# Four small instructions of a recurrent-attention-plus-MLP kernel move from GpSimd to ScalarE

## The chip, the core and the metric

The kernel runs on one NeuronCore of a Trainium2 chip. The core's engines each work through a queue of their own, in order, and meet through semaphores: TensorE (PE in the profile; PEld is its weight load), VectorE (DVE), ScalarE (ACT), GpSimd (POOL) and SyncE (SP), which here only issues DMAs. The metric is the time of one execution on the device in microseconds (us).

## The reference

The first half is a recurrence with a decay for every channel, over four batches, eight heads, 768 time steps and 48 channels a head. The second half is an MLP whose activation is the maximum of two products.

```python
for t in range(S):
    cur = np.einsum('bhd,bhe->bhde', u[None] * kt, vt)
    y[:, :, t] = np.einsum('bhd,bhde->bhe', rt, state + cur)
    state = wt[:, :, :, None] * state + np.einsum('bhd,bhe->bhde', kt, vt)
...
h1 = x @ w1          # x: the 3072 rows of y, 384 wide
h2 = x @ w2          # 1024 wide
return (np.maximum(h1, h2) @ w_out).astype(np.float32)
```

## The kernel before

**Units.** The work is cut into eight units (line 39). A unit is 256 time steps of one batch (units 0 to 3, the first third of the sequence) or of two batches (unit 4: batches 0 and 1, second third; unit 5: batches 2 and 3, second third; units 6 and 7: the last third). A partition holds two neighbouring time steps, so 128 partitions hold the 256 steps, and the lower and upper 64 partitions are two chunks of 128 steps.

**A unit's steps**, by the names in the order list (`name.unit.rest`, with `@a`, `@d`, `@p` for ScalarE, VectorE, GpSimd where there is a choice):

- `load` brings w, k, r and v in. `wp` multiplies the decays of a partition's two steps, `ln` takes the logarithm (ScalarE), and `ex` sums the logarithms over time by a matmul with a triangular matrix. For units 3 to 7 that matmul runs in f16 in two parts: `hi` is the logarithm times 256, rounded to f16, and `lo` is what the rounding left, 256 times the logarithm minus `hi` (VectorE, line 398). `hi` and `lo` are written into slices of the tile that is named wst.
- `e0` and `ie` are the exponentials of the sums, `rk`, `ru`, `dg`, `dd` and `di` make the diagonal with u in it, `rw` and `kw` multiply decays into r and k, and `scale` makes the scaled r and k (tiles rp and kp). `tr` and `te` turn them (TensorE, then a ScalarE copy into the tile RK); from unit 5 on a DMA does it (`dt`).
- `kv` is the matmul of k with v, `st` adds it to the f32 state S_f, and `sm` multiplies the state with the chunk's decay, whose exponential is `we` (tile W). `sb.n.0` and `sb.n.1` round the state to bf16 for TensorE, tile S_b, one for partitions 0 to 63 and one for 64 to 127: the half-partition copies.
- `sc` is the matmul of scaled k with scaled r, `mk` copies it under a triangular mask into the tile M (VectorE, line 635), `ya` is the matmul of M with v, `yi` that of the state S_b with r, and `xe` takes the result out of PSUM.
- `gt`, `rl`, `op`, `oe` and `os` are the MLP: the matmul with w1 - w2 (line 691), relu, the matmuls with w2 @ w_out and w_out (lines 709 and 713), the copy out of PSUM and the store. The maximum of h1 and h2 is taken as relu(h1 - h2) + h2.

**What sets the order.** No scheduler is at work. The list `ORDER` (line 51) is walked once, and each step issues its instructions to the queues of its engines at that place. A wait arises where an instruction needs what another engine writes, or writes over what another still reads.

**Buffers.** In PSUM two pairs of banks, named Y, serve `kv`, `sc` and the outputs `ya`/`yi` in turn, so an `sc` waits until `mk` has read an earlier one. Four banks named G serve everything else. The tiles rku and T exist once.

**The functions in question.** `sb` (line 606) makes one instruction through the helper `copy` (line 165): 64 partitions, 192 elements each for a unit of one batch, 768 for one of two batches that carries state on. `hi` (line 392) makes one through the helper `times` (line 196): line 198 on ScalarE, line 200 on GpSimd or VectorE.

Of the kernel before, what the change touches and what calls it, by code (L numbers as in the profile page):

```python
# [53 lines left out]
mz.0.1 e0.0.1 load.0.r rw.0.0@d ex.0.0 zero.M.1@p mz.0.0 ie.0.0 ie.0.1 kw.0.0@p identb@p wt.0.0  # L54
rw.0.1@p wt.0.1 load.1.w.0 u we.0.0 identq@a uspread hot.8.3 e0.0.0 wp.1.0@p ln.1.0 ex.1.0
zero.k.1@p rk.0.0@d utake@a ru.0.0@p load.1.r rw.1.0@p load.1.v vb.1.0@a zero.M.2@p load.0.v
scale.0.1.0.0@d scale.0.1.0.1@d scale.0.0.0.0@d tr.0.0.0 vb.0.0@a vb.0.1@a kv.0 st.0.0@a sb.0.0@p
scale.0.0.0.1@d tr.0.0.1 mz.1.0 ie.1.0 dg.0 dd.0@p we.0.1 load.1.k rk.1.0@d st.0.1 kw.1.0@d ru.1.0@d
wt.1.0 di.0.0@d te.0.0.0@a hot.8.5 sc.0.0.0.0 sc.0.0.1.0 we.1.0 vb.1.1@a te.0.0.1@a hot.8.4
sc.0.0.0.1 wload.1.2 w2turn.2.0 wload.0.1 e0.1.0 zero.M.0@p sm.0@p scale.1.0.0.0@d dg.1 load.2.w.0  # L60
# [16 lines left out]
scale.4.0.0.0@d load.4.v vb.4.0@a ie.4.0 ya.2.0.1.0 vb.4.1@a yi.2.0 op.1.0 xe.2.0@a op.0.1 oe.0.1@a  # L77
ru.4.0@d scale.4.1.0.0@d tr.4.0.1 dg.4 sc.3.0.1.0 mk.3.0.1.0 sc.3.0.0.0 mk.3.0.0.0 oe.1.0@a
load.5.w.0 gt.2.0 rl.2.0@a load.3.v vb.3.1@a gt.2.3 rl.2.3@a gt.2.1 rl.2.1@a te.4.0.1@a vb.3.0@p
kv.3 st.3.0@a gt.2.2 scale.4.1.1.0@p kv.4 rl.2.2@a row.4 wp.5.0@p ln.5.0 hi.5@p dd.4@d di.4.0@d  # L80
di.4.1@d wl.3 load.5.r sb.3.0@a we.3 st.3.1 os.1.1 load.5.k sm.3@p os.0.1 load.5.v st.4.0 sb.4.0@p
rk.5.1@p ru.5.1@p tr.4.1.0 te.4.1.0@a tr.4.0.0 te.4.0.0@a op.0.0 tr.4.1.1 load.6.w.0 wp.6.0@p lo.5@d
st.4.1 rk.5.0@d ya.3.0.1.0 ex.5.1 ya.3.0.0.0 te.4.1.1@a sc.4.1.0.0 mk.4.1.0.0 sb.3.1@a yi.3.0
xe.3.0@a oe.0.0@a mz.5.1 ex.5.0 mz.5.0 op.2.1 oe.2.1@a sc.4.1.1.0 mk.4.1.1.0 sc.4.0.1.0 mk.4.0.1.0
# [18 lines left out]
xe.6.1@a ya.6.0.0.0 ya.6.0.1.0 op.5.0 scale.7.0.1.0@d dg.7 dt.7.0.1 xe.6.0@a gt.6.0 rl.6.0@d gt.6.1  # L103
rl.6.1@d gt.6.4 rl.6.4@a sm.5@p scale.7.1.1.0@p dt.7.1.1 scale.7.1.0.0@p gt.6.2 rl.6.2@d dd.7@d
vb.7.1@a gt.6.3 oe.5.0@a rl.6.3@a gt.6.6 gt.6.7 di.7.1@d rl.6.6@d gt.6.5 rl.6.5@d vb.7.0@a kv.7
st.7.0 sb.7.0@p sc.7.1.0.0 mk.7.1.0.0 rl.6.7@a op.6.0 sc.7.1.1.0 mk.7.1.1.0 dt.7.0.0 os.4.0 dt.7.1.0
op.6.2 sc.7.0.1.0 di.7.0@d mk.7.0.1.0 os.5.2 sc.7.0.0.0 mk.7.0.0.0 op.6.1 oe.6.1@d os.6.1 ya.7.1.0.0
ya.7.1.1.0 ya.7.0.0.0 ya.7.0.1.0 sb.7.1@a oe.6.0@d os.6.0 yi.7.0 yi.7.1 xe.7.0@a op.6.3 oe.6.3@a
os.6.3 os.5.3 os.5.0 oe.6.2@a xe.7.1@d gt.7.0 gt.7.7 rl.7.7@d rl.7.0@a gt.7.2 gt.7.1 rl.7.2@d gt.7.4
# [669 lines left out]
```

## Time and profile before

| | |
|---|---|
| three timed runs | 156.62, 158.8 and 159.0 us, median 158.8 |
| profiled execution | span 156.0 us from its first to its last instruction; the profile has no other time of this execution |
| busy: PE | 140.7 us, 90% of the span |
| busy: DVE | 124.1 us, 80% |
| busy: ACT | 90.0 us, 58% |
| busy: POOL | 90.4 us, 58% |
| mean granted TensorE clock | 0.985 of full speed |

The profile shows one execution. A line of the timeline is start, duration, engine, source line, operation, output <- inputs, shapes, and xN where N equal instructions follow each other; in brackets stands how long the engine was idle before it and who released it. Helpers carry the line, so line 166 is every copy on any engine and line 174 or 178 every product on VectorE or GpSimd; one goes by the tiles' names.

### The profile page before, as it was taken

How to read it: one execution, taken by the hardware profiler on the slowest of the kernel's cores; microseconds unless marked ns; L12 is line 12 of the kernel's file. 1: busy time of each engine (PE TensorE's matmuls, PEld its weight loads, DVE VectorE, ACT ScalarE, POOL GpSimd, SP SyncE). 2: the span in 40 equal slices, each digit the busy share in tenths (PEclk: the TensorE clock that was granted, in tenths of full speed). 3: DMA queues.
4: the chain of work that ended last, by engine and by line, in shares of the span. 5: the costliest groups of instructions: out<-in, count | busy, mean ns of one | idle time of the engine just before them, and what ended most of it. 6: DMA issues, size and time to landing. Idle time of an engine off the chain costs nothing.

```text
span 156.0 us, 5548 instructions
## 1 busy us (share of the span) xinstructions
PE 140.7 (90%) x2401; PEld 85.9 (55%) x2404; DVE 124.1 (80%) x161; ACT 90.0 (58%) x165; POOL 90.4 (58%) x105
## 2 busy tenths in 40 slices
PE   4899987998899989793499999999999999999991
PEld 1364645666667758561365645665556646574560
DVE  4690997999979999499989995997889987854610
ACT  3253735779979896964069689544763673023111
POOL 7949389891734975599529579486099932000000
PEclk9999999999999999999779999999999999999998
DMA  4999997999999679996098399869989298024033
GB/s 107 305 299 365 312 327 234 326 284 344 266 244 280 169 175 334 220 254 190 1 218 238 66 194 237 228 182 152 264 195 252 52 135 200 4 103 153 0 128 131
DMA packets 71187, 31.85 MB, mean 204 GB/s; under 512 B 66293, under 2 KB 70390, under 8 KB 71162
## 3 DMA queue, kind: packets, MB, share of 16 engines
q1 hardware_dynamic: 71162, 31.49, 77.3%
q8 instruction: 19, 0.31, 0.9%
q14 instruction: 6, 0.05, 0.1%
HBM read 23.61 MB, written 4.73 MB: 182 GB/s over the span
## 4 chain that ended last, share of the span: by engine, by line
PE 63%; DVE 16%; ACT 6%; issue 5%; POOL 5%; DMA 3%; SPq 1%; DVEq 0%; POOLq 0%; ACTq 0%
PE G L691 19%; PE G L713 16%; PE G L709 7%; DVE rku L174 6%; PE Y L626 4%; PE G L232 3%; PE Y L673 3%; DMA lr<-in_r_dram 3%; DVE M L635 2%; PE Y L660 2%; ACT RK L166 2%; PE Y L581 2%; POOL wst L200 1%; PE G L305 1%; POOL kp L174 1%
## 5 line engine op out<-in xcount | busy, mean ns | idle before, releaser
L691 PE MATMUL G<-xT,wd_sb 128*128 128x256 bf16 (+1 forms) x192 | 35.3, 335 | 0.7 <-ACT xT L166 0.7
L713 PE MATMUL G<-wo_sb,gT 128*128 128x384 bf16 x192 | 35.1, 326 | 0.0
L635 DVE CAST_PREDICATED M<-mask,Y 128x1024 bf16<-128x1024 int32 (+1 forms) x26 | 28.9, 1135 | 3.7 <-PE Y L626 3.6
L701 ACT ACTIVATE gT<-G 128x512 bf16<-128x512 f32 x37 | 21.0, 603 | 18.4 <-PE G L691 18.4
L691 PEld LDWEIGHTS <-wd_sb 128*128 128x128 bf16 x192 | 18.8, 101 | 13.6 <-DVE M L501 0.7
L713 PEld LDWEIGHTS <-gT 128*128 128x128 bf16 x192 | 18.7, 98 | 12.5 <-ACT gT L701 0.2
L178 POOL TENSOR_TENSOR kp<-lk,iE 128x384 bf16<-128x384 f32 x16 | 18.2, 1161 | 8.3 <-issue 4.0
L232 PE MATMUL G<-S_b 128*128 128x512 bf16 x45 | 14.6, 469 | 2.2 <-DVE S_b L261 2.1
L178 POOL TENSOR_TENSOR rku<-rku,u_b 128x384 f32<-128x384 f32 x14 | 14.0, 1025 | 4.0 <-DVE rku L174 2.2
L166 ACT COPY osb<-G 128x384 f32<-128x384 f32 x17 | 8.1, 481 | 13.7 <-PE G L713 13.4
L709 PE MATMUL G<-wc_sb,xT 128*128 128x384 bf16 x72 | 15.7, 328 | 0.0
L166 ACT CAST xT<-Y 128x768 bf16<-128x768 f32 x10 | 10.1, 1020 | 9.8 <-PE Y L660 8.2
L174 DVE TENSOR_TENSOR rku<-lr,lk 128x768 f32<-128x768 f32 x9 | 15.3, 1712 | 0.0
L626 PE MATMUL Y<-RK 48*64 48x128 bf16 x384 | 9.8, 226 | 5.1 <-DVE M L635 4.5
L166 ACT COPY RK<-G 128x1024 bf16<-128x1024 bf16 x12 | 12.0, 1026 | 1.7 <-PE G L550 1.6
L626 PEld LDWEIGHTS <-RK 48*64 48x64 bf16 x384 | 6.3, 108 | 10.5 <-issue 9.9
L425 DVE TENSOR_TENSOR MZ<-G,lg 128x384 f32<-128x384 f32 (+1 forms) x13 | 6.7, 521 | 6.0 <-PE G L383 5.1
L174 DVE TENSOR_TENSOR rp<-lr,G 128x768 bf16<-128x768 f32 (+2 forms) x13 | 10.5, 824 | 0.9 <-ACT G L421 0.6
L487 DVE TENSOR_REDUCE dg<-rku 128x16 f32<-128x768 f32 x12 | 11.0, 946 | 0.0
L178 POOL TENSOR_TENSOR lk<-lk,lw 128x384 f32<-128x384 f32 x6 | 7.3, 1226 | 5.5 <-DVE rku L174 5.5
L703 DVE TENSOR_SCALAR gT<-G 128x512 bf16<-128x512 f32 x11 | 7.4, 690 | 3.8 <-PE G L691 3.8
L232 PEld LDWEIGHTS <-S_b 128*128 128x128 bf16 x48 | 5.0, 114 | 9.6 <-issue 4.4
(102 smaller groups left out, 241.1 us busy)
## 6 DMA issues: line engine op xcount, KB each, us to landing
lk<-in_k_dram SPq DMA_DIRECT2D x12, 384.0 KB, 5.8
lr<-in_r_dram SPq DMA_DIRECT2D x12, 384.0 KB, 6.4
lv<-in_v_dram SPq DMA_DIRECT2D x12, 384.0 KB, 6.4
out_dram<-osb SPq DMA_DIRECT2D x24, 192.0 KB, 2.1
lw<-in_w_dram SPq DMA_DIRECT2D x11, 384.0 KB, 5.1
gT<-in_moe_w_dram SPq DMA_DIRECT2D x4, 512.0 KB, 6.0
wso<-in_moe_w_out_dram SPq DMA_DIRECT2D x4, 384.0 KB, 6.0
wst<-in_moe_w_dram SPq DMA_DIRECT2D x2, 512.0 KB, 5.6
```

Of the source, the lines that this page charges most:

```text
L166: (nc.scalar.copy if e == "a" else nc.vector.tensor_copy if e == "d" else nc.gpsimd.tensor_copy)(o, i)
L174: op(o, a, b)
L178: op(o[:, g], a[:, g], b[:, g])
L232: nc.tensor.matmul(t, zz[:, 0:P], zz[:, 0:512], start=True, stop=True)
L487: nc.vector.reduce_sum(s.dg[:, b].rearrange("p i h -> p h i"), s.rku[:, b], axis=AX.X)
L626: nc.tensor.matmul(t[q * Q:(q + 1) * Q, e, p * P:(p + 1) * P].rearrange("s (i g) -> s i g", i=2), s.kT[d, b, j, y * n + p, q, :], s.rT[d, ...
L635: nc.vector.copy_predicated(t[:, :, 2 * n * y:2 * n * (y + 1)].rearrange("s i (p e) g -> s p e i g", e=2), mask[:, j].bitcast(I32).unsquee ...
L691: nc.tensor.matmul(t[:, m * n * P:(m + 1) * n * P].rearrange("c (b t) -> c b t", t=P), wd_sb[:, ko, fo * P:(fo + 1) * P], s.xT[:, 0:n, ko, :],
L701: nc.scalar.activation(o, i, AF.Relu)
L703: nc.vector.tensor_scalar_max(o, i, 0.0)
L709: nc.tensor.matmul(t[:, 0:HD], s.xT[:, a, ko, :], wc_sb[:, ko, :], start=(ko == 0), stop=False)
L713: nc.tensor.matmul(t[:, 0:HD], s.gT[:, c:c + P], wo_sb[:, f, :], start=False, stop=(f == FO - 1))
```

## The change

Four steps change their engine, from GpSimd to ScalarE, and keep their place in the list: `sb.0.0`, `hi.5`, `sb.4.0` and `sb.7.0`. All other copies of the state were on ScalarE already, and of the other roundings `hi` three are on ScalarE and that of unit 7 on VectorE. Two of the four changed lines of the list:

```diff
-kv.3 st.3.0@a gt.2.2 scale.4.1.1.0@p kv.4 rl.2.2@a row.4 wp.5.0@p ln.5.0 hi.5@p dd.4@d di.4.0@d
-di.4.1@d wl.3 load.5.r sb.3.0@a we.3 st.3.1 os.1.1 load.5.k sm.3@p os.0.1 load.5.v st.4.0 sb.4.0@p
+kv.3 st.3.0@a gt.2.2 scale.4.1.1.0@p kv.4 rl.2.2@a row.4 wp.5.0@p ln.5.0 hi.5@a dd.4@d di.4.0@d
+di.4.1@d wl.3 load.5.r sb.3.0@a we.3 st.3.1 os.1.1 load.5.k sm.3@p os.0.1 load.5.v st.4.0 sb.4.0@a
```

The order on TensorE, VectorE and SyncE is the same as before. On GpSimd, at the place where units 3, 4 and 5 meet (wst is the target of `hi.5`, S_f of `sm.3`, S_b of `sb.4.0`, rku of `rk.5.1` and `ru.5.1`):

```order
 L178 TENSOR_TENSOR kp_74<-lk,iE 128x8x48 x2
 L178 TENSOR_TENSOR lg<-lw 128x384 x2
-L200 TENSOR_SCALAR wst<-lg 128x768
 L174 TENSOR_TENSOR S_f<-T,W 128x192
-L166 CAST S_b<-S_f 64x2x8x48
 L178 TENSOR_TENSOR rku<-lr,lk 128x384 x2
 L178 TENSOR_TENSOR rku<-rku,u_b 128x384 x2
```

Two instructions are gone, and the products of unit 5 follow on `sm.3`. On ScalarE at the same place (gT is a relu, lg the logarithm `ln.5`, W the exponential `we.3`, RK the three copies `te.4.1.0`, `te.4.0.0`, `te.4.1.1`):

```order
 L701 ACTIVATE gT<-G 128x512
 L372 ACTIVATE lg<-lg 128x768
+L198 ACTIVATE wst<-lg 128x768
 L166 CAST S_b<-S_f 64x4x48
 L473 ACTIVATE W<-WL 128x4
+L166 CAST S_b<-S_f 64x2x8x48
 L166 COPY RK<-G 128x4x256 x3
 L166 CAST S_b<-S_f 64x4x48
```

Here `hi.5` stands directly behind the logarithm and ahead of `we.3`, and `sb.4.0` ahead of the three copies. On ScalarE near the end of unit 7 (the second gT row is `rl.6.7`, the last relu of unit 6; the last S_b row is `sb.7.1`):

```order
 L701 ACTIVATE gT<-G 128x512
 L166 CAST vp_77<-lv 128x8x2x48
+L166 CAST S_b<-S_f 64x2x8x48
 L701 ACTIVATE gT<-G 128x512
 L166 CAST S_b<-S_f 64x2x8x48
```

`sb.7.0` now stands ahead of `rl.6.7`. In the first units, `sb.0.0` stands on ScalarE directly behind the copy `st.0.0` that it reads; on GpSimd it had stood ahead of `dd.0`.

More of the change, by code (lines that the diff above doesn't have):

```diff
@@ L56 @@
 zero.k.1@p rk.0.0@d utake@a ru.0.0@p load.1.r rw.1.0@p load.1.v vb.1.0@a zero.M.2@p load.0.v
-scale.0.1.0.0@d scale.0.1.0.1@d scale.0.0.0.0@d tr.0.0.0 vb.0.0@a vb.0.1@a kv.0 st.0.0@a sb.0.0@p
+scale.0.1.0.0@d scale.0.1.0.1@d scale.0.0.0.0@d tr.0.0.0 vb.0.0@a vb.0.1@a kv.0 st.0.0@a sb.0.0@a
 scale.0.0.0.1@d tr.0.0.1 mz.1.0 ie.1.0 dg.0 dd.0@p we.0.1 load.1.k rk.1.0@d st.0.1 kw.1.0@d ru.1.0@d
@@ L105 @@
 vb.7.1@a gt.6.3 oe.5.0@a rl.6.3@a gt.6.6 gt.6.7 di.7.1@d rl.6.6@d gt.6.5 rl.6.5@d vb.7.0@a kv.7
-st.7.0 sb.7.0@p sc.7.1.0.0 mk.7.1.0.0 rl.6.7@a op.6.0 sc.7.1.1.0 mk.7.1.1.0 dt.7.0.0 os.4.0 dt.7.1.0
+st.7.0 sb.7.0@a sc.7.1.0.0 mk.7.1.0.0 rl.6.7@a op.6.0 sc.7.1.1.0 mk.7.1.1.0 dt.7.0.0 os.4.0 dt.7.1.0
 op.6.2 sc.7.0.1.0 di.7.0@d mk.7.0.1.0 os.5.2 sc.7.0.0.0 mk.7.0.0.0 op.6.1 oe.6.1@d os.6.1 ya.7.1.0.0
```

## The prediction

> **What bounds the kernel now.** I read the busy shares first, then the waits, then the chain of work that ended last, and then the timeline around the longest wait.
>
> ```profile
> PE 140.7 (90%) x2401; PEld 85.9 (55%) x2404; DVE 124.1 (80%) x161; ACT 90.0 (58%) x165; POOL 90.4 (58%) x105
> PE 63%; DVE 16%; ACT 6%; issue 5%; POOL 5%; DMA 3%; SPq 1%; DVEq 0%; POOLq 0%; ACTq 0%
> ...
> PE Y L626 <- DVE M L635: 4.5, 1, 4.5
> ```
>
> TensorE is busy for 90% and carries 63% of the chain; ScalarE and GpSimd are idle for 42%, so a moved instruction matters only where somebody waits behind it. The last row is TensorE's longest wait for another engine: one wait of 4.5 us for VectorE's masked copy. The chain leads into it over GpSimd:
>
> ```profile
> 64.24 2.14 POOL wst L200
> ```
>
> `hi.5`, a moved step, holds 2.14 us of the chain. The timeline of the stretch, VectorE and GpSimd:
>
> ```profile
> 64.24 2.13 POOL L200 TENSOR_SCALAR wst<-lg 128x768 f16<-128x768 f32 x1 [3.46 <-ACT lg L372]
> 66.34 0.50 POOL L174 TENSOR_TENSOR S_f<-T,W 128x192 f32<-128x192 f32 x1
> 66.40 1.26 DVE L398 SCALAR_TENSOR_TENSOR wst<-lg,wst 128x768 f16<-128x768 f32 x1 [2.27 <-POOL wst L200]
> 66.80 1.54 POOL L166 CAST S_b<-S_f 64x768 bf16<-64x768 f32 x1
> 67.58 0.55 DVE L600 TENSOR_TENSOR T<-Y,S_f 128x384 f32<-128x384 f32 x1
> 68.05 6.85 DVE L174 TENSOR_TENSOR rku<-lr,lk 128x768 f32<-128x768 f32 x1
> 68.31 1.96 POOL L178 TENSOR_TENSOR rku<-lr,lk 128x384 f32<-128x384 f32 x2
> 70.23 1.95 POOL L178 TENSOR_TENSOR rku<-rku,u_b 128x384 f32<-128x384 f32 x2
> 72.13 1.95 POOL L178 TENSOR_TENSOR lg<-lw 128x384 f32<-128x384 f32 x2
> 74.82 1.21 DVE L635 CAST_PREDICATED M<-mask,Y 128x1024 bf16<-128x1024 int32 x1
> ```
>
> `lo.5` (L398) waits 2.27 us for `hi.5`. Then `rk.5.0`, the 6.85 us product, starts during `sb.4.0` on GpSimd (L166) and ends 0.82 us after the last of six GpSimd products, at 74.90. The same kind of product takes 0.95 us elsewhere (quoted below), so it did its work only once the six were over: GpSimd's queue locked it out. TensorE and its clock meanwhile:
>
> ```profile
> 76.08 0.52 PE L626 MATMUL Y<-RK 48*64 48x128 bf16 x16 [4.47 <-DVE M L635]
> 76.53 2.74 PE L691 MATMUL G<-xT,wd_sb 128*128 128x256 bf16 x12
> 79.76 1.48 PE L691 MATMUL G<-xT,wd_sb 128*128 128x256 bf16 x12
> ...
> 72.86:76.27 3.41, 0.19 (x13) 0.18 (x15) 3.41 (x3) 0.00 (x0) 2.52 (x4) 1.00 0.03 10
> 76.27:79.68 3.41, 3.41 (x44) 2.13 (x35) 2.95 (x4) 0.97 (x2) 0.67 (x1) 0.50 0.26 67
> ```
>
> The third `sc` of unit 4 waits from 71.6 (76.08 less 4.47) for the mask copy behind `rk.5.0`. In the last two rows (a stretch, its length, busy time of PE, PEld, DVE, ACT, POOL, granted clock, DMA) TensorE is busy for 0.19 us of 3.41, and in the 3.41 us after it the clock is 0.50: twelve matmuls take 2.74 us that take 1.48 us next time. From 76.08 to the end the chain is TensorE without a gap worth naming, so what this stretch gives or takes reaches the end.
>
> **The change, part by part.** ScalarE around the place, and what the moved forms cost there and elsewhere:
>
> ```profile
> 63.27 0.88 ACT L372 ACTIVATE lg<-lg 128x768 f32<-128x768 f32 x1
> 64.00 0.35 ACT L166 CAST S_b<-S_f 64x192 bf16<-64x192 f32 x1
> 64.24 0.22 ACT L473 ACTIVATE W<-WL 128x4 f32<-128x4 f32 x1
> 64.58 1.93 ACT L166 COPY RK<-G 128x1024 bf16<-128x1024 bf16 x2
> 67.26 1.01 ACT L166 COPY RK<-G 128x1024 bf16<-128x1024 bf16 x1 [0.75 <-PE G L550]
> ...
> 87.59 0.84 ACT L198 ACTIVATE wst<-lg 128x768 f16<-128x768 f32 x1
> 88.90 0.95 DVE L398 SCALAR_TENSOR_TENSOR wst<-lg,wst 128x768 f16<-128x768 f32 x1
> 89.76 0.95 DVE L174 TENSOR_TENSOR rku<-lr,lk 128x768 f32<-128x768 f32 x1
> ```
>
> *`hi.5`.* On ScalarE it starts at 64.18, when the logarithm is done (63.27 + 0.88), and takes 0.84 us as `hi.6` does: done at 65.02 instead of 66.37. `lo.5` takes 0.95 us where nothing disturbs it: done at 66.0 instead of 67.66. `we.3` now follows `hi.5` and the short S_b copy, done at 65.4. `sm.3` needs it; it meets `lo.5` and ends, if it has to stand back for it, at 66.4 instead of 66.85. `st.4.1` (L600) waits for `sm.3` and takes 0.55: `rk.5.0` is issued at 67.0 instead of 68.05.
>
> *`sb.4.0`.* GpSimd loses 1.54 us, so its six products start behind `sm.3` at 66.4 instead of 68.31. On ScalarE the copy takes 0.83 us like `sb.7.1` (row at 130.33 below), and starts at 65.3, behind `we.3`; its input, `st.4.0`, comes in VectorE's queue ahead of `lo.5`, which VectorE reached early enough to stand idle for 2.27 us, so by 64.2.
>
> *What ScalarE pays.* The two steps, which overlap their neighbours by some 0.1 us each, put 1.42 us ahead of the three RK copies: these start at 66.0 instead of 64.58. The 0.75 us for which ScalarE stood idle ahead of the third, and a little more between rows, take most of it up; at 0.91 us from one to the next the third ends at 68.83 instead of 68.27. The first `sc` of unit 4, which reads it, and all of TensorE's work up to the stall follow 0.56 us later. TensorE so reaches its wait at 72.1 instead of 71.6.
>
> *The stall.* Everything hangs on when VectorE does `rk.5.0`. Bounds come from rows: as soon as one product on GpSimd is over, or when all six are. For the first:
>
> ```profile
> 80.91 2.68 POOL L178 TENSOR_TENSOR kp<-lk,iE 128x384 bf16<-128x384 f32 x2 [3.97 <-issue]
> 81.02 1.70 DVE L174 TENSOR_TENSOR rku<-rku,u_b 128x768 f32<-128x768 f32 x1
> ...
> 90.79 2.34 POOL L178 TENSOR_TENSOR rku<-rku,u_b 128x384 f32<-128x384 f32 x2 [2.19 <-DVE rku L174]
> 92.36 1.32 DVE L501 TENSOR_TENSOR M<-identq,gd 128x512 int32<-128x512 int32 x1
> 93.10 2.40 POOL L178 TENSOR_TENSOR rku<-lr,lk 128x384 f32<-128x384 f32 x2
> ```
>
> At 81.02 and 92.36 a VectorE product was issued while GpSimd ran a product with another queued behind it. Both times VectorE went next (1.70 and 1.32 us, 0.75 and 0.64 us of them waiting) and GpSimd's queued one was stretched. The one that was locked out for six had been issued behind a one-input copy, `sb.4.0`, which the change takes away. I take the nearer rows: `rk.5.0`, issued at 67.0 during the first product, gets in at 67.4 and ends at 68.2. The first mask copy is then bound by its `sc` (69.3) and done at 70.6, before TensorE asks for it at 72.1. The stall is gone: 76.08 - 72.1 = **-4.0 us**. With no empty stretch the clock stays at 1.00: 2.74 - 1.48 = **-1.3 us**. At the other bound the six products end at 72.2, `rk.5.0` at 73.0, the mask copy at 74.2: -1.9 us for the stall, and the idle 2.1 us no longer fill a stretch of 3.41, so -1.3 us again.
>
> What is late next is VectorE's row of mask copies, each 1.21 us; they keep ahead of TensorE, since they move earlier with the matmuls they read. The loads that follow were issued long before.
>
> On the page "SBUF — State Buffer", section "SBUF: two separate sides", the Trainium skill says that VectorE with two SBUF inputs and GpSimd share a port pair, that whoever starts first holds it for the whole instruction, and that the other is fully blocked. By that rule `rk.5.0` would wait for one GpSimd instruction, which is the first bound; the 6.85 us row, through six, is more than the rule gives, and the rows at 81.02 and 92.36 agree with it.
>
> *`sb.7.0`, unit 7.*
>
> ```profile
> 128.61 0.62 ACT L701 ACTIVATE gT<-G 128x512 bf16<-128x512 f32 x1
> 130.33 0.83 ACT L166 CAST S_b<-S_f 64x768 bf16<-64x768 f32 x1 [1.10 <-DVE S_f L597]
> ...
> 130.29 1.46 PE L713 MATMUL G<-wo_sb,gT 128*128 128x384 bf16 x8
> ```
>
> `sb.7.0` adds a wait for the state at 130.33, and behind it is `rl.6.7`, which ran at 128.61. It would now run from 131.05 to 131.67. The last of the eight matmuls of `op.6.0` reads it; eight in 1.46 us, with 0.33 for one (its group's mean is 326 ns), put its start at 131.42, and its weight load stands 0.15 ahead: **+0.4 us** on TensorE, to the end. `sb.7.1` behind it ends near 132.4, and `yi.7`, which reads it, comes after two more `op` of some 1.9 us each.
>
> *`sb.0.0`, first units.* ScalarE's next steps come 0.4 us later, among them `e0.1.0`, for which a VectorE product waits.
>
> ```profile
> 22.69 0.53 ACT L372 ACTIVATE lg<-lg 128x384 f32<-128x384 f32 x1 [2.40 <-POOL lg L174]
> 24.22 0.56 DVE L425 TENSOR_TENSOR MZ<-G,lg 128x384 f32<-128x384 f32 x1 [1.02 <-PE G L383]
> ```
>
> ScalarE's idle 2.40 us and VectorE's 1.02 us hide it; if that cover fails it costs 0.4 us. GpSimd loses one short copy ahead of `dd.0`; I count no gain, since its next work waits for VectorE. I take **+0.2**, between 0 and 0.4.
>
> Sum: -4.0 - 1.3 + 0.4 + 0.2 = **-4.7 us**, a span of 151.3.
>
> **The rivals.**
>
> *B, the lockout stays.* `rk.5.0` again waits for all six products. For it speaks its own row; against it that the copy before it is gone. -1.9 - 1.3 + 0.4 + 0.2 = -2.6: span 153.4.
>
> *C, the lockout moves, the slower side.*
>
> ```profile
> 95.81 2.36 DVE L635 CAST_PREDICATED M<-mask,Y 128x1024 bf16<-128x1024 int32 x2 [0.68 <-PE Y L626]
> ...
> 97.37 1.98 POOL L178 TENSOR_TENSOR lr<-lr,lw 128x384 f32<-128x384 f32 x2
> ```
>
> Eight GpSimd products of unit 6 run from 90.79 to 97.37 + 1.98 = 99.35 without a gap. If VectorE's `di.5` (92.36) is locked out there, it ends at 99.9 (0.6 behind them) instead of 93.7, 6.2 us late. VectorE's time up to the mask copies of unit 5 (95.81 - 93.68, less one 0.55 us step) holds 1.6 us of idling, so they, and TensorE with them, are some 4.7 us late; the empty stretch brings the slow clock, 1.3: +6.0. Behind the forecast that is +1.3 (157.3); behind B it is +3.4, slower than before. It decides when GpSimd's first product beats `di.5` to the port. Against it: in the row at 92.36 VectorE got in, and both engines move earlier together.
>
> *D, nothing changes.* ScalarE could be the bound that hides the gain; but its third RK copy (68.83) would have to come at 73 for that.
>
> **How the numbers follow.** The median of the runs, 158.8, lies 2.8 us above the profiled span and the fastest 0.6 above. The forecast is the median minus 4.7: 154.1 us. B gives 156.2, C 160.1 (151.3 + 6.0 + 2.8) or 162.2, D about 159. A measurement of this kernel tells some 2% from no change, 3.2 us. Chances: forecast 0.50, B 0.27, C 0.20, D 0.03. Faster by over 2% (under 155.6): 0.48 of the forecast and 0.05 of B, 0.53. Slower (over 162.0): 0.13 from C, which reaches it behind B. Within 2%: the rest, 0.34. The range starts at 151.3, the forecast's span, as if a run added nothing to it; it ends where the milder C does, 160.1. It leaves out 0.13 above and a few hundredths below.
>
> **What would show it.** `lo.5` starting near 65.1 shows the first step; a VectorE product in rku under 2 us near 67 and no wait of TensorE over 1 us between 71 and 77 show the stall gone; a granted clock of 1.00 there shows the second term; `rl.6.7` behind S_b and a gap before the eighth matmul of `op.6.0` the third. The prediction is wrong if VectorE shows another product of several microseconds beside GpSimd's, in unit 5 or 6.

## The result, and the profile after

| | before | after |
|---|---|---|
| median of the runs, four each | 158.23 us (156.62 to 159.0) | 153.01 us (151.94 to 154.71) |
| span of the profiled execution | 156.0 us | 150.2 us |
| mean granted TensorE clock | 0.985 | 0.973 |

The ratio is 0.968, with a 95% interval of 0.958 to 0.978: faster. Ratios, here and below, leave out runs over 1.5% above the fastest of the same kernel, a slower state; medians are of all runs. The forecast was 154.1 us, and 151.3 for the span.

The mean clock fell although the half clock at the changed place is gone: the changed kernel's profile has 6.83 us at half clock from 9.06 us on, in the first units, and that of before has none there. Over the fourteen traces of this case, of both kernels and the twelve experiments, it is 0, 3.41 or 6.83 us there (3.41 in e8, which differs from the changed kernel in one exchange near the end), so it isn't put down to the change.

From the page of the changed kernel: the busy shares, the chain that ended last by engine, and TensorE's longest wait in the line that had carried the 4.5 us.

```profile
PE 139.2 (93%) x2404; PEld 84.3 (56%) x2404; DVE 118.3 (79%) x161; ACT 92.4 (62%) x169; POOL 87.2 (58%) x101
PE 74%; ACT 12%; POOL 3%; DMA 3%; issue 3%; DVE 2%; SPq 1%; DVEq 0%; ACTq 0%; POOLq 0%
...
PE Y L626 <- ACT RK L166: 0.7, 1, 0.7
```

The wait for VectorE's mask copy is gone; 0.7 us for ScalarE's copy into RK is left in that line. VectorE's share of the chain fell from 16% to 2%, ScalarE's rose from 6% to 12%. The timeline of the place where units 3, 4 and 5 meet, on ScalarE, VectorE and GpSimd, after the change:

```profile
62.54 0.88 ACT L372 ACTIVATE lg<-lg 128x768 f32<-128x768 f32 x1
63.46 0.84 ACT L198 ACTIVATE wst<-lg 128x768 f16<-128x768 f32 x1
64.56 0.82 ACT L166 CAST S_b<-S_f 64x768 bf16<-64x768 f32 x1
65.28 2.81 ACT L166 COPY RK<-G 128x1024 bf16<-128x1024 bf16 x3
64.40 0.96 DVE L398 SCALAR_TENSOR_TENSOR wst<-lg,wst 128x768 f16<-128x768 f32 x1 [0.99 <-ACT wst L198]
66.24 1.27 DVE L174 TENSOR_TENSOR rku<-lr,lk 128x768 f32<-128x768 f32 x1
74.88 1.64 DVE L174 TENSOR_TENSOR rku<-rku,u_b 128x768 f32<-128x768 f32 x1
65.69 2.66 POOL L178 TENSOR_TENSOR rku<-lr,lk 128x384 f32<-128x384 f32 x2
72.14 1.97 POOL L178 TENSOR_TENSOR lk<-lk,lw 128x384 f32<-128x384 f32 x2
74.70 2.69 POOL L178 TENSOR_TENSOR kp<-lk,iE 128x384 bf16<-128x384 f32 x2 [0.60 <-POOL lk L178]
```

`hi.5` takes 0.84 us on ScalarE instead of 2.13 on GpSimd, the state copy 0.82 instead of 1.54. About 0.7 of the 1.54 can be put down to a wait beside VectorE's `lo.5`: where nothing disturbs it the copy takes 0.82 on GpSimd too (row at 68.09 of e10 below). `rk.5.0` takes 1.27 us where it took 6.85: it waits for one GpSimd product, and the second of that pair stands back for it (two take 2.66 instead of 1.96). The row at 74.88 is `ru.5.0`, VectorE's next product of two SBUF operands; the experiments turn on it.

Where TensorE stands at the same instructions, before and after (the first fence is of before, the second of after, and its last two rows are stretches with length, busy time of PE, PEld, DVE, ACT, POOL, and granted clock):

```profile
71.19 0.42 PE L626 MATMUL Y<-RK 48*64 48x128 bf16 x16
...
81.17 0.42 PE L673 MATMUL Y<-M,vp 64*32 64x128 bf16 x32
...
131.68 0.42 PE L626 MATMUL Y<-RK 48*64 48x128 bf16 x16
...
151.28 1.46 PE L713 MATMUL G<-wo_sb,gT 128*128 128x384 bf16 x8
```

```profile
68.14 0.31 PE L626 MATMUL Y<-RK 48*64 48x128 bf16 x8 [0.71 <-ACT RK L166]
...
71.01 0.64 PE L626 MATMUL Y<-RK 48*64 48x128 bf16 x32
71.59 1.48 PE L691 MATMUL G<-xT,wd_sb 128*128 128x256 bf16 x12
...
74.77 0.42 PE L673 MATMUL Y<-M,vp 64*32 64x128 bf16 x32
...
123.89 1.76 PE L713 MATMUL G<-wo_sb,gT 128*128 128x384 bf16 x8
125.58 0.42 PE L626 MATMUL Y<-RK 48*64 48x128 bf16 x16
...
145.52 1.46 PE L713 MATMUL G<-wo_sb,gT 128*128 128x384 bf16 x8
...
68.20:71.61 3.41, 3.41 (x66) 2.05 (x67) 2.28 (x4) 2.11 (x4) 3.41 (x5) 1.00 0.72 174
71.61:75.02 3.41, 3.41 (x76) 2.66 (x72) 3.41 (x4) 3.02 (x5) 2.81 (x4) 1.00 0.94 257
```

| TensorE reaches | before | after | ahead by | gained since the row above |
|---|---|---|---|---|
| the second `sc` of unit 4 | 71.19 | 71.01 | 0.18 | 0.18 |
| the twelve `gt` behind the third `sc` | 76.53 | 71.59 | 4.94 | 4.76, mostly the wait of 4.47 |
| the first `ya` of unit 4 | 81.17 | 74.77 | 6.40 | 1.46, the half clock |
| `op.6.0`, its eight matmuls | 130.29 | 123.89 | 6.40 | 0 |
| the `sc` of unit 7 behind it | 131.68 | 125.58 | 6.10 | -0.30 |
| the last eight matmuls | 151.28 | 145.52 | 5.76 | -0.34 |

All but 0.18 us of the gain is made within 11 us. TensorE is busy for all of 3.41 us in both stretches at the place, and the clock stays at 1.00.

### The profile page after: what moved, and what is told of

Same layout as the page of the kernel before. It is cut to its first block, busy times and chain, and to the rows that moved or that the text cites. A ratio compares the mean times of both kernels' runs of the same rounds, so it can differ in the third digit from the quotient of the medians.

```text
span 150.2 us, 5551 instructions
## 1 busy us (share of the span) xinstructions
PE 139.2 (93%) x2404; PEld 84.3 (56%) x2404; DVE 118.3 (79%) x161; ACT 92.4 (62%) x169; POOL 87.2 (58%) x101
## 4 chain that ended last, share of the span: by engine, by line
PE 74%; ACT 12%; POOL 3%; DMA 3%; issue 3%; DVE 2%; SPq 1%; DVEq 0%; ACTq 0%; POOLq 0%
PE G L691 20%; PE G L713 19%; PE G L709 8%; ACT RK L166 4%; PE Y L626 4%; PE Y L673 4%; PE G L232 4%; DMA lr<-in_r_dram 3%; PE Y L660 3%; PE G L316 3%; ACT gT L701 2%; PE G L550 2%; ACT S_b L166 2%; POOL kp L174 1%; PE G L305 1%
## 5 line engine op out<-in xcount | busy, mean ns | idle before, releaser
L691 PE MATMUL G<-xT,wd_sb 128*128 128x256 bf16 (+1 forms) x192 | 34.0, 326 | 0.7 <-ACT xT L166 0.7
L691 PEld LDWEIGHTS <-wd_sb 128*128 128x128 bf16 x192 | 18.2, 98 | 12.9 <-DVE M L501 0.7
L166 ACT CAST S_b<-S_f 64x192 bf16<-64x192 f32 (+1 forms) x16 | 9.4, 587 | 1.8 <-DVE S_f L597 1.6
L174 DVE TENSOR_TENSOR rku<-lr,lk 128x768 f32<-128x768 f32 x9 | 9.7, 1090 | 0.3 <-DVE S_f L174 0.3
```

The source lines that it names most:

```text
L166: (nc.scalar.copy if e == "a" else nc.vector.tensor_copy if e == "d" else nc.gpsimd.tensor_copy)(o, i)
L174: op(o, a, b)
L691: nc.tensor.matmul(t[:, m * n * P:(m + 1) * n * P].rearrange("c (b t) -> c b t", t=P), wd_sb[:, ko, fo * P:(fo + 1) * P], s.xT[:, 0:n, ko, :],
```

## The experiments

Every ratio is to the kernel before on the same chip, with its 95% interval. Steps are named as in the list.

### Which of the four steps: e1, e2, e3, e4

e1 moves `sb.4.0` alone, e2 `hi.5` alone, e3 both, e4 `sb.0.0` and `sb.7.0`.

```diff
e1  -st.4.0 sb.4.0@p
    +st.4.0 sb.4.0@a
e2  -ln.5.0 hi.5@p
    +ln.5.0 hi.5@a
e3  both of these
e4  -st.0.0@a sb.0.0@p      and  -st.7.0 sb.7.0@p
    +st.0.0@a sb.0.0@a           +st.7.0 sb.7.0@a
```

> The kernel before with one of the four steps moved: sb.4.0 on ScalarE, hi.5 left on GpSimd. Theory of the copy (VectorE's rk.5.0 is locked out only when it is issued behind the one-input copy sb.4.0): hi.5 still ends near 66.4, rk.5.0 is issued near 67.9 while GpSimd runs a two-input product, waits for that one alone and takes 1.2 to 1.8 us; TensorE has no wait over 1 us between 71 and 77 and the clock there is 1.00; 4 to 5.5 us faster than before. Theory of the load (rk.5.0 waits for the whole queue of six products, whatever stands ahead of it, and the gain is the time taken off GpSimd): the six end 1.5 us earlier, rk.5.0 takes over 4 us, TensorE still waits some 3 us; 1.5 to 2.8 us faster.

> The kernel before with one of the four steps moved: hi.5 on ScalarE, sb.4.0 left on GpSimd. Theory of the copy: lo.5 comes 1.3 to 2 us earlier, but rk.5.0 is again issued during sb.4.0, is locked out until the six products end near 72.5, and takes about 6 to 7 us; TensorE still waits some 2 to 3 us; 1.5 to 3 us faster than before. Theory of the load: the six end 1.6 us earlier, with nearly the same numbers in time, 1.5 to 3 us faster; so this run tells the two apart only together with the one that moves sb.4.0 alone. Theory that hi.5 is the whole cause (lo.5's wait of 2.3 us starts the lateness): rk.5.0 under 2 us, 4.5 us faster or more.

> The kernel before with hi.5 and sb.4.0 on ScalarE, sb.0.0 and sb.7.0 left on GpSimd. Theory: all of the change's gain without its cost at the end, so op.6.0's eight matmuls take 1.46 us again instead of 1.76; 0.3 to 0.6 us faster than the changed kernel, 5.5 to 6.5 us faster than before. Rival (the first and last copies cost nothing): like the changed kernel, 5.0 to 5.8 us faster.

> The kernel before with only sb.0.0 and sb.7.0 on ScalarE. Theory: rk.5.0 of 6.9 us and the 4.5 us wait stay; op.6.0's eight matmuls take 1.7 to 1.9 us instead of 1.46; 0.3 to 0.6 us slower than before. Rival (they cost nothing): the same time as before within 0.2 us.

| | steps on ScalarE | median | ratio |
|---|---|---|---|
| e1 | `sb.4.0` | 152.88 us | 0.958 [0.947, 0.968] |
| e2 | `hi.5` | 157.09 us | 0.995 [0.990, 1.000] |
| e3 | `hi.5`, `sb.4.0` | 152.44 us | 0.963 [0.955, 0.971] |
| e4 | `sb.0.0`, `sb.7.0` | 158.44 us | 0.997 [0.991, 1.002] |

One copy of 64 partitions is the whole gain: e1, e3 and the change can't be told apart. The 0.3 to 0.6 us that were expected of e3 and e4 are less than these ratios tell. The timeline of e1, VectorE, GpSimd and TensorE:

```profile
69.77 1.30 DVE L174 TENSOR_TENSOR rku<-lr,lk 128x768 f32<-128x768 f32 x1
76.75 1.76 DVE L174 TENSOR_TENSOR rku<-rku,u_b 128x768 f32<-128x768 f32 x1
80.74 1.18 DVE L174 TENSOR_TENSOR lr<-lr,lw 128x768 f32<-128x768 f32 x1
...
75.74 1.95 POOL L178 TENSOR_TENSOR lk<-lk,lw 128x384 f32<-128x384 f32 x2
80.28 0.82 POOL L166 CAST vp<-lv 128x768 bf16<-128x768 f32 x1
...
73.46 1.48 PE L691 MATMUL G<-xT,wd_sb 128*128 128x256 bf16 x12
```

`lo.5` still waits its 2.26 us for `hi.5` here, and the run loses nothing by it: that wait was on the chain of before, but behind it stood the lockout. e2, where `hi.5` is fast and the copy stays, shows the reverse (VectorE, GpSimd, TensorE, then three stretches as above):

```profile
65.10 6.81 DVE L174 TENSOR_TENSOR rku<-lr,lk 128x768 f32<-128x768 f32 x1
...
64.54 0.81 POOL L166 CAST S_b<-S_f 64x768 bf16<-64x768 f32 x1
...
73.10 0.64 PE L626 MATMUL Y<-RK 48*64 48x128 bf16 x16 [3.53 <-DVE M L635]
73.67 2.74 PE L691 MATMUL G<-xT,wd_sb 128*128 128x256 bf16 x12
76.34 0.64 PE L626 MATMUL Y<-RK 48*64 48x128 bf16 x16
76.92 2.29 PE L691 MATMUL G<-xT,wd_sb 128*128 128x256 bf16 x12
...
68.36:71.77 3.41, 1.21 (x22) 0.60 (x20) 3.41 (x1) 1.36 (x3) 2.74 (x3) 1.00 0.74 209
71.77:75.18 3.41, 2.08 (x24) 1.48 (x24) 3.41 (x6) 0.01 (x1) 1.95 (x2) 0.50 0.00 2
75.18:78.59 3.41, 3.41 (x30) 2.17 (x29) 2.61 (x3) 2.03 (x3) 0.54 (x1) 0.50 0.91 233
```

`rk.5.0` is issued earlier and locked out as long, 6.81 us. The 1.5 to 3 us that were expected did not come: the wait is 0.94 us shorter, but now two stretches run at half clock instead of one, so that the second twelve `gt` take 2.29 us too (0.81 more than 1.48). The stretch ahead of the two has 1.21 us of TensorE's work, so it need not be empty. In e4 the lockout (6.84 us) and the 4.5 us stay, two stretches run at half clock as in e2, and the eight matmuls of `op.6.0` take 1.76 us as after the change; in e3, with `sb.7.0` back on GpSimd, they take 1.46.

### The tail: e8

The changed kernel with `rl.6.7` ahead of `sb.7.0`.

```diff
-st.7.0 sb.7.0@a sc.7.1.0.0 mk.7.1.0.0 rl.6.7@a op.6.0
+st.7.0 rl.6.7@a sb.7.0@a sc.7.1.0.0 mk.7.1.0.0 op.6.0
```

> The changed kernel with one pair of ScalarE's steps exchanged: rl.6.7 stands ahead of sb.7.0 again. If the 0.3 us by which op.6.0's eight matmuls grew (1.46 to 1.76) are the wait for rl.6.7 behind sb.7.0, they take 1.46 again and the run is 0.3 us faster than the changed kernel's 153.0 (ratio to before 0.965). If the state copy itself is what they wait for, they stay at 1.76 or the gap moves to yi.7.

ScalarE in the changed kernel, then TensorE in e8:

```profile
123.93 0.83 ACT L166 CAST S_b<-S_f 64x768 bf16<-64x768 f32 x1 [1.60 <-DVE S_f L597]
124.67 0.58 ACT L701 ACTIVATE gT<-G 128x512 bf16<-128x512 f32 x1
```

```profile
123.65 1.46 PE L713 MATMUL G<-wo_sb,gT 128*128 128x384 bf16 x8
```

The 0.30 us are the wait for `rl.6.7` behind the copy's own wait for the state. The span is 149.7 us. Its four runs lie between 150.1 and 153.1 us and can't tell 0.3 us, so it stands on the row alone.

### Is it the copy, or GpSimd's time: e9

All four steps on GpSimd as before; only the place of the copy in GpSimd's queue differs.

```diff
-st.4.0 sb.4.0@p
-rk.5.1@p ru.5.1@p tr.4.1.0
+st.4.0
+rk.5.1@p ru.5.1@p sb.4.0@p tr.4.1.0
```

> The kernel before, with all four steps still on GpSimd and nothing added or taken away; only sb.4.0 is issued behind the four products of rk.5.1 and ru.5.1 instead of ahead of them. Theory A, it is the one-input copy under way on GpSimd when rk.5.0 is issued that locks the product out: rk.5.0 now comes beside a product, takes 1.2 to 1.8 us instead of 6.85, TensorE's wait of 4.5 us is gone, the clock is 1.00 there, and the run is 4.5 to 6 us faster (ratio 0.96 to 0.97) although GpSimd does as much as before. Theory B, it is GpSimd's 1.54 us of work that has to go: GpSimd's queue is as long as before, rk.5.0 takes over 5 us, the wait stays over 2.5 us, and the ratio is 0.985 to 1.00.

157.3 to 159.5 us, ratio 1.005 [0.999, 1.011]: no gain. Neither theory foresaw how (VectorE, GpSimd, TensorE of e9):

```profile
68.40 1.28 DVE L174 TENSOR_TENSOR rku<-lr,lk 128x768 f32<-128x768 f32 x1
75.39 7.13 DVE L174 TENSOR_TENSOR rku<-rku,u_b 128x768 f32<-128x768 f32 x1
...
75.12 1.98 POOL L178 TENSOR_TENSOR lk<-lk,lw 128x384 f32<-128x384 f32 x2
...
84.89 1.12 PE L709 MATMUL G<-wc_sb,xT 128*128 128x384 bf16 x3 [3.73 <-DVE osb L166]
85.80 2.58 PE L713 MATMUL G<-wo_sb,gT 128*128 128x384 bf16 x8
```

`rk.5.0` comes in after one product, as theory A said. Then `ru.5.0` is locked out for 7.13 us by the products behind it. Through `dg.5` and a copy out of PSUM, which stand behind it on VectorE, TensorE waits for 3.73 us, with the slow clock after it. The lockout has moved on by one VectorE product. It is issued 0.27 us after GpSimd began the first `lk` product; in e1 that is 1.01 us, when the second is under way, and it takes 1.76. The copy's 0.82 us in GpSimd's queue, ahead of the `lk` products, makes this difference.

### The same from the other side: e5, e7

e5 leaves the four steps on GpSimd and puts `rk.5.0` ahead of `lo.5`; e7 does so with `hi.5` and `sb.4.0` on ScalarE.

```diff
-wp.6.0@p lo.5@d
-st.4.1 rk.5.0@d ya.3.0.1.0
+wp.6.0@p rk.5.0@d lo.5@d
+st.4.1 ya.3.0.1.0
```

> The kernel before, with all four steps still on GpSimd; only rk.5.0 stands ahead of lo.5 in VectorE's queue, where VectorE idles for 2.27 us from 64.13. GpSimd starts hi.5, an instruction with one input, at 64.24. Theory A (a VectorE product is locked out when it is issued during a one-input instruction of GpSimd): if rk.5.0 is issued ahead of hi.5 it takes 0.95 us, lo.5 starts at 66.4 as before, TensorE's wait is gone and the run is 4.5 to 6 us faster (ratio 0.96 to 0.97); if it is issued during hi.5 it stays out until GpSimd first pauses, lo.5 is late behind it and the run is no faster (ratio 0.99 to 1.02). Theory C (the copy sb.4.0 is peculiar, not the kind of instruction): rk.5.0 takes under 3 us either way, and the run is 4 us or more faster.

> hi.5 and sb.4.0 on ScalarE (0.963 of before), sb.0.0 and sb.7.0 on GpSimd, and rk.5.0 ahead of lo.5 in VectorE's queue, where VectorE idles for 1 us. rk.5.0 takes 0.95 us near 63.4 beside nothing on GpSimd. If ru.5.0 meets GpSimd at a product kp, as in the changed kernel, it takes 1.6 to 1.8 us, no wait of TensorE is over 1 us, and the ratio is 0.955 to 0.965, no better than without the exchange, as the chain runs over TensorE and ScalarE there. If the products of unit 5, which now start undisturbed, run so that ru.5.0 is issued during the first lk product, as in the run with rk.5.0 early and the copy on GpSimd, it is locked out for over 6 us and the ratio is 0.98 to 1.00.

VectorE in e5:

```profile
64.99 0.95 DVE L174 TENSOR_TENSOR rku<-lr,lk 128x768 f32<-128x768 f32 x1
...
76.59 6.42 DVE L174 TENSOR_TENSOR rku<-rku,u_b 128x768 f32<-128x768 f32 x1
```

`rk.5.0` is free of GpSimd, and again `ru.5.0` is locked out, which neither theory foresaw. Ratio 0.988 [0.967, 1.008], the gain mostly gone. In e7 `ru.5.0` meets a `kp` product, as after the change, and takes 1.64 us; median 152.39 us, ratio 0.954 [0.944, 0.963], which can't be told from e1's or the change's own.

### What makes VectorE wait for many: e10, e11, e12

Every product that had been locked out by then was issued while GpSimd ran an instruction that itself had waited for VectorE. e10 takes that wait off `sb.4.0` and off the first `lk` product by small copies ahead of them; e11 puts such a wait on the first product of `rk.5.1` in e1. e12 makes `sb.4.0` a product with ones.

```diff
e10 +nc.gpsimd.tensor_copy(t[:, 0:1], S_f[0:1, 1, 0, 0, 0:1])   # ahead of sb.4.0
    +nc.gpsimd.tensor_copy(t[:, 0:1], rku[0:1, 0, 0, 0, 0:1])   # ahead of kw.5.0
e11 +nc.vector.memset(rku[0:1, 1, 0, 0, 0:1], 0.0)              # ahead of rk.5.1
e12 -nc.gpsimd.tensor_copy(o, i)                                # sb.4.0
    +nc.gpsimd.tensor_mul(o, i, ones)
```

> The kernel before, all four steps still on GpSimd, with extra work of two GpSimd copies of one element each (results unused): one ahead of sb.4.0, one ahead of the products lk of unit 5 (kw.5.0). Each reads what VectorE wrote, so the wait for VectorE stands at the small copy and no longer at sb.4.0 or at the first lk product. Theory E, a VectorE product is locked out through the queue when the GpSimd instruction under way had itself waited for VectorE (so in every lockout seen, 6.4 to 7.1 us, and in no product that got in): rk.5.0 and ru.5.0 now take under 2.2 us each, TensorE's waits of over 2 us around 71 to 85 are gone, and the run is 4.5 to 6 us faster (ratio 0.96 to 0.97) although GpSimd does more than before. Theory A, it is the kind of sb.4.0, a copy with one input: rk.5.0 takes 6.8 us again and the ratio is 0.99 to 1.01. Theory F, it is chance or the phase of the queue: rk.5.0 or ru.5.0 is locked out for over 6 us, whichever.

> The kernel with sb.4.0 alone on ScalarE (0.958 of before), with extra work of one VectorE memset of one element of rku, during VectorE's idle stretch, which makes the first product of rk.5.1 on GpSimd wait for VectorE by its semaphore (long fulfilled when it is reached). Theory E: rk.5.0, issued during that product, is locked out through the queue for over 5 us, TensorE waits for over 2 us, and most of the gain is lost (ratio 0.98 to 1.00). Theory A or F: rk.5.0 takes about 1.3 us as without the memset, and the ratio stays at 0.95 to 0.97.

> The kernel before, sb.4.0 on GpSimd at its old place, but as a product of the state with ones (two inputs in SBUF) in place of the copy; extra work of one small VectorE memset for the ones at the start. The product takes about 1.9 us instead of 0.82 (128x384 takes 1.0), so GpSimd has about 1.1 us more. Theory A, it is the kind of sb.4.0, a copy with one input, that locks rk.5.0 out: rk.5.0, issued near 68 during the new product, gets in behind it and takes 1.5 to 3 us, TensorE's wait shrinks from 4.5 to under 1.5 us; as GpSimd's queue is then as in the run with the copy behind the products, ru.5.0 may be locked out in its turn, so the ratio may be anything from 0.96 to 1.00. Theory P, it is the place (what is queued behind, and the moment of the issue), not the kind: rk.5.0 takes 7 to 8 us and the wait stays over 4 us, ratio 1.00 to 1.01.

GpSimd and VectorE of e10, VectorE of e11, and GpSimd and VectorE of e12:

```profile
68.09 0.82 POOL L166 CAST S_b<-S_f 64x768 bf16<-64x768 f32 x1
68.48 6.97 DVE L174 TENSOR_TENSOR rku<-lr,lk 128x768 f32<-128x768 f32 x1
```

```profile
68.11 1.28 DVE L174 TENSOR_TENSOR rku<-lr,lk 128x768 f32<-128x768 f32 x1
```

```profile
69.43 2.17 POOL L614 TENSOR_TENSOR S_b<-S_f,ones 64x768 bf16<-64x768 f32 x1
70.67 2.71 DVE L176 TENSOR_TENSOR rku<-lr,lk 128x768 f32<-128x768 f32 x1
78.76 3.98 DVE L176 TENSOR_TENSOR rku<-rku,u_b 128x768 f32<-128x768 f32 x1
```

Theory E falls on both sides: without the wait `rk.5.0` is locked out for 6.97 us (ratio 0.998 [0.993, 1.003]), and with it it takes 1.28 us (0.950 [0.944, 0.956]). In e12 `rk.5.0` lets the long product and one more pass (2.71 us), and `ru.5.0`, issued during the first `lk` product, lets four instructions pass (3.98 us). Ratio 0.983 [0.971, 0.996], between the two ends: "one or all" isn't the rule. All three runs are as theory A, the kind of `sb.4.0`, forecast them; what speaks against it is in other rows.

Over the fourteen traces, from 20 us on, VectorE issued 107 instructions with two SBUF operands while GpSimd ran an instruction with the next directly behind it (by at most 0.15 us). 98 of them waited for one GpSimd instruction at most. The other nine let two to seven pass: all six that were issued during the `sb.4.0` of unit 4 on GpSimd, and all three issued during the first `lk` product of unit 5. One-input copies into vp let VectorE in as soon as they were done (in e1 the row at 80.74, 1.18 us, issued during the copy at 80.28), and the `lk` products have two inputs. So the kind of instruction under way doesn't decide it alone, though in e12 another kind, which is also a longer instruction, let VectorE in after two and not seven.

Nor is it chance from one execution to the next: where the order around the place is the same, so is `rk.5.0`, 6.84 to 6.85 us in before, e4 and e6, and 1.26 to 1.27 us in the changed kernel, e3 and e8. What decides it, the place in the queue or the moment of the issue for example, is open.

### The clock: e6

Sixteen more matmuls fill TensorE's wait.

```diff
-mk.4.1.1.0 sc.4.0.1.0
+mk.4.1.1.0 hot.16.9 sc.4.0.1.0
```

> The kernel before with extra work: 16 matmuls whose result nobody reads stand ahead of the third sc of unit 4, so that TensorE works during part of its wait of 4.5 us. The wait for VectorE's mask copy ends where it ended. If the half clock of 3.41 us behind the wait comes from TensorE's idling, the clock stays at 1.00, the first twelve matmuls of the stretch take 1.48 instead of 2.74 us, and the run is about 1.3 us faster than before (ratio 0.99). If the half clock has another cause, the twelve take 2.74 us and the ratio is 1.00 or above.

TensorE in e6 (fifteen of the sixteen are in the records):

```profile
69.98 3.63 PE L232 MATMUL G<-S_b 128*128 128x512 bf16 x15
74.55 0.42 PE L626 MATMUL Y<-RK 48*64 48x128 bf16 x16 [0.95 <-DVE M L635]
74.90 1.49 PE L691 MATMUL G<-xT,wd_sb 128*128 128x256 bf16 x12
```

The lockout is as long as before (6.85 us), but the twelve `gt` take 1.49 us and not 2.74, at a clock of 1.00. So the half clock of before came from TensorE's idling and is a cost of its own: from the third `sc` to the first `ya` it is 3.83 us (78.38 - 74.55) instead of 5.09. The ratio, 0.999 [0.991, 1.008], doesn't resolve 1.3 us. The page "TensorE: Matmul & The Clock Gate" of the Trainium skill, in Part 1, has the clock halve after an idle window of about 3.4 us; here a stretch with 0.19 us of work in 3.41 was enough, and in e2 one with 1.21, so by these traces the window need not be idle.

## Why the prediction was right, step by step

- **What bounds the kernel: right.** The lockout of `rk.5.0` was the term that mattered. e1 takes it away alone and has the whole gain.
- **`hi.5`: durations right, of little worth.** 0.84 us on ScalarE as forecast, and `lo.5` follows 0.94 us behind its start and takes 0.96. The prediction let it pay by an earlier issue of `rk.5.0`, and the chain gave it 2.14 us; but e2 gains 0.5%, and e1 without it no less than the change.
- **What ScalarE pays: right.** From the logarithm's start to that of the RK copies it is 1.43 us more than before (65.28 - 62.54 against 64.58 - 63.27; forecast 1.42), and the third copy's end loses 0.55 (forecast 0.56): 68.09 less 68.27 is -0.18, and the logarithm had started 0.73 earlier. Those 0.73 come from ahead of the place and were not forecast; part is a wait of TensorE of 0.54 us for a kp product on VectorE, near 58 in before, which is absent. That product takes 1.26 us instead of 1.76, as GpSimd runs its copy into vp when it is issued, held up by a late load of v, and not a kp product. It is so in e2 too, but not in e3 or e8, so it is put down to chance and not to the change.
- **The stall: -4.0 forecast; 4.76 gained behind the second `sc`, less 0.55 for ScalarE, is -4.2.** **The clock: -1.3 forecast, -1.46 measured**; the sum had counted the twelve `gt` (1.26) and left out the `sc` at half clock beside them (0.62 instead of 0.42). The reason given for -1.3 at the other bound, that 2.1 us of idling no longer fill a stretch of 3.41, is not borne out: in e2 the half clock followed a stretch in which TensorE idled for 2.20 us.
- **The tail: +0.4 forecast, +0.30 measured**, with its cause as forecast (e8). **The first units: +0.2 taken, nothing seen**: the cover held. ScalarE's idle time of 2.40 us is 1.79 there and the logarithm behind it starts at 22.63 us, where it had started at 22.69; and e4, which has both steps, can't be told from before.
- **The sum: -4.7 forecast, -5.8 in the span.** -4.2, -1.46 and +0.30 make -5.4; the 0.73 that came from ahead, less 0.34 us that TensorE lost to a gap in its issue near 131, make up the rest. That the span came 1.1 us lower than forecast is thus in good part chance. The runs give -5.2. In every run whose span is known the time is 1.7 to 1.9 us over the span, so the 2.8 us that the prediction read between median and profiled span were in part scatter between executions, and the lower end of its range, 151.3, asked for a run with nothing over the span.
- **The rivals.** B, the same lockout again, did not come. C, that the lockout moves, was real as a mechanism but misplaced: not `di.5` beside unit 6's products, which took 1.31 us, but `ru.5.0` beside unit 5's, in e9, e5 and e12. The change escapes it because GpSimd, rid of the copy, has its `lk` products behind it (72.14 to 74.11) when `ru.5.0` is issued at 74.88.
- **The step that failed is a reason:** "The one that was locked out for six had been issued behind a one-input copy, `sb.4.0`, which the change takes away." It named the right instruction, but being a one-input copy is not the cause: one-input copies into vp let VectorE in (e1), and two-input `lk` products lock it out (e9, e5, e12). Had the change put the copy behind the products instead, the same reasoning would have forecast a gain of 5 us, and there is none.

On the Trainium skill's page "SBUF — State Buffer", section "SBUF: two separate sides", a GpSimd instruction that starts first holds the shared ports for its whole length and VectorE is blocked for that long. 98 of the 107 places agree with a wait for one instruction; the nine others took 2.7 to 7.1 us, and the one in the kernel before cost most of what the change gains.

## What to carry to other kernels

A VectorE instruction several times longer than its like elsewhere, beside a back-to-back run on GpSimd, is likely a lockout and not work; look for such rows first, and ask which of VectorE's next products would be issued into the rest of that run. Moving one 0.8 us instruction off GpSimd was worth 5 us or more (e1), moving it to another place on GpSimd nothing: only a trace of the new order shows where VectorE's issue falls. An idle stretch of TensorE can cost its length and then one or two stretches at half clock (before and e2), so price both, with every matmul in it.

## What was not expected of the hardware

- A waiting VectorE product can be passed by seven GpSimd instructions in a row (7.13 us in e9) or by two (e12), or wait for one (e1). What decides this was not found; the wait for VectorE on the GpSimd instruction under way (e10, e11) is ruled out.
- GpSimd's rounding of 128x768 to f16 takes 2.13 us, its copy of 64x768 to bf16 0.82; on ScalarE they take 0.84 and 0.82.
- The half clock came for two stretches of 3.41 us in a row in e2, although TensorE was busy for 2.08 us of the first, and for 1.21 us of the stretch ahead of them.
